# Transposing x on TensorE for three batches, and issuing the first pass's stores from SP

## The chip, the cores and the metric
The kernel runs on one core of a Trainium2 chip. The metric is the device time of one execution in microseconds: 1576.8 us before, the median of three runs (1575.4 to 1581.59). The core has five engines with an instruction stream each: TensorE (PE) for matmuls, VectorE (DVE), ScalarE (ACT), GpSimd (POOL) and SyncE (SP), which here only issues DMAs. A DMA is issued by an instruction in the stream of SP or of ACT and moved by 16 DMA engines. PSUM is the memory that PE writes; SBUF is the other on-chip memory.

## The reference
```python
# attention: x (8, 8, 512, 64), state (8, 8, 32, 64), scale = 1/8
a      = softmax(scale * x @ state^T)          # over the 32 states
xread  = a @ state
a2     = softmax(scale * state @ x^T)          # over the 512 tokens
sread  = a2 @ x
t = concat([xread, sread], axis=2)             # (8, 8, 544, 64) -> (4352, 512)
# gated layer, 512 -> 1536 -> 512
y = (sigmoid(t @ w_gate) * (t @ w_val)) @ w_out
# second layer, 512 -> 2048 -> 512
out = relu(y @ w_in)**2 @ w_out2
```
All arrays are float32; the large weights arrive as 64-bit floats, read as pairs of 32-bit words.

## The kernel before, in words
**Precision.** A float32 operand is split into a high part, rounded to PE's fast format by ACT, and a low part, the difference, by DVE. A product is three matmuls (`mm3`, L190 to L192): high by high, high by low, low by high.

**Weights.** A weight tile comes as raw 64-bit words (`load_raw`, SP, L116, three buffers) and is converted (`convert`): one ACT instruction (L126), five DVE instructions (L128 to L144), an ACT cast (L147) and a DVE subtraction (L148).

**Attention, first half.** For a batch b and a group g of four heads, `load_x` brings x in 32 x 32 blocks by four DMAs of 128 B runs: ACT issues them for batch 0, SP for the others. `a2` transposes the blocks on DVE (L292) into `xf`, so that the 64 features stand on partitions, and splits the result (L293 ACT, L294 DVE). `a3` multiplies it with a diagonal arrangement of the states (PSUM tile `ps_s`), and `a4` makes the softmax over the states: transposes on DVE, exponential on ACT, and the split result `a` (L332, L333). The tiles `xf` and `a1` share one SBUF buffer. The raw x tile `xq` has one buffer.

**The gated layer uses the states' product.** Since xread is a @ state, the product state @ [w_gate, w_val] is formed once for each chunk of two feature tiles (`state_weights`, L452, PSUM pair `ps_g`), copied out (`go`, L456 and L460, three buffers), and stored to DRAM by four DMAs (`store_g`, L468). This is done in two passes over the six chunks: the first (m=0) for batches 0 to 3, the second (m=1) for batches 4 to 7. The first pass's stores are issued by ACT, the second's by SP. For each batch and chunk `load_g` (SP, L512) reads it back, `split_gw` splits it (L520 ACT, L521 POOL), and `front_x` multiplies it with `a` into `psg` and `psv`. A sigmoid (ACT, L537) and a product (DVE, L543) follow, and `back1` accumulates with w_out into `acc`.

**PSUM.** `acc` has four banks, `mm` two, and `at` two. `at` is shared by `ps_st`, `ps_s`, `ps_g` and, later, the transposes of the second softmax (`ps_e`, `ps_sr`, `ps_so`).

**Order.** The work is written in units (batch, feature tile) of six steps. `spread` gives every piece of side work a due step: the attention of batch 0 is written before the first unit, that of batches 1, 2 and 3 in units 1 to 4, 4 to 8 and 8 to 12; the second group of states in unit 23.5. A planner in the framework then orders the instructions of each engine by their priority in the written order and by its own modelled times, and inserts the waits. Each engine runs its list in order, and a DMA issue in that list waits like any other instruction.

The four issuing lines:
```python
# load_x (L258)
(nc.scalar if b == 0 else nc.sync).dma_start(out=..., in_=...)
# store_g (L468)
(nc.sync if m else nc.scalar).dma_start(
    out=to[:, :, i, :], in_=o[NS * r : NS * (r + 1)]
)
```

Of the kernel before, what the change touches and what calls it, by code (L numbers as in the profile page):

```python
# [8 lines left out]
F32 = mybir.dt.float32  # L9
# [9 lines left out]
P = 128  # L19

FC = 2

QB = 4

PAD_L, PAD_R = 144, 160

# [5 lines left out]
def kernel(  # L32
# [21 lines left out]
    nc = tc.nc  # L54
    B, H, S, D = x.shape
    NS = state.shape[2]
# [8 lines left out]
    NT = S // P  # L65
# [19 lines left out]
    at_p = ctx.enter_context(tc.tile_pool(name="at", bufs=2, space=PSUM))  # L85
# [7 lines left out]
    xs_p = one.enter_context(tc.tile_pool(name="xsp", bufs=1, side="right"))  # L93
    aa_p = gen.enter_context(tc.tile_pool(name="aa", bufs=QB, side="right"))
    wr_p = gen.enter_context(tc.tile_pool(name="wr", bufs=2, side="right"))
# [5 lines left out]
    ident = pad_p.tile([P, P], F32, name="ident")  # L101
# [70 lines left out]
    def width(b):  # L172
        return S if b < B else NSTATE
# [11 lines left out]
    }  # L185
    p_dram = {b: dram.tile([P, KD, S], F32, name=f"pd{b}") for b in range(QB)}
    y_dram = {b: dram.tile([P, KD, width(b)], F32, name=f"yd{b}") for b in blocks}
# [19 lines left out]
    xq_p = att.enter_context(tc.tile_pool(name="xq", bufs=1))  # L207
    xn_p = att.enter_context(tc.tile_pool(name="xn", bufs=1))
    xx_p = att.enter_context(tc.tile_pool(name="xx", bufs=2))
    f_p = att.enter_context(tc.tile_pool(name="f2k", bufs=2))  # L210
# [38 lines left out]
    loaded_x, loaded_xn = {}, {}  # L249
    by_pair = x.rearrange("b (g j k) s d -> b g j k s d", g=2, j=2)  # L250

    def load_x(b, g):

        t = xq_p.tile([P, 2, S], F32, tag="xq", name="xq")
        for q in range(4):
            j, e = divmod(q, 2)
            src = by_pair[b, g, j, :, :, 32 * e : 32 * (e + 1)]
            (nc.scalar if b == 0 else nc.sync).dma_start(  # L258
                out=t[32 * q : 32 * (q + 1)].rearrange("i c (J a) -> i (c J) a", a=32),
                in_=src.rearrange("c (J i) a -> i (c J) a", i=32),  # L260
            )
        loaded_x[b, g] = t

# [12 lines left out]
    def group_stages(b, g):  # L276

        v = {}
        busy = b < QB

        def lx():
            load_x(b, g)

        def ln():
            load_xn(b, g)

        def a2(p):
            def run():
                xf = f_p.tile([P, S], F32, tag="xf", name="xf", bufs=1)
                h = xx_p.tile([P, S], F32R, tag="xth", name="xth")  # L290
                l = xx_p.tile([P, S], F32R, tag="xtl", name="xtl")
                nc.vector.transpose(xf, loaded_x[b, g][:, p, :])  # L292
                nc.scalar.copy(out=h, in_=xf)  # L293
                nc.vector.tensor_sub(out=l, in0=xf, in1=h.bitcast(F32))  # L294
                v["xt", p] = (h, l)

            return run
# [104 lines left out]
        def b7():  # L402
# [12 lines left out]

        return {
            "LX": lx, "LN": ln, "LS": ls, "A20": a2(0), "A21": a2(1), "A3": a3, "A4": a4, "SX0": sx(0), "SX1": sx(1),
            "B4": b4, "B5": b5, "B60": b6(0), "B61": b6(1), "B7": b7,
        }
# [8 lines left out]
    def attention(b):  # L428
        gs = [group_stages(b, g) for g in range(2)]
        pick = lambda names: [  # L430
            (lambda: None) if n == "-" else gs[int(n[-1])][n[:-2]] for n in names
        ]
        return [lambda: prep_diag(b), *pick(ORDER_A)], pick(ORDER_B)
# [29 lines left out]
    def store_g(ch, c, m):  # L463
        g, i = divmod(c, 2)
        o = g_out.pop((ch, c, m))
        for r in range(BM):
            to = g_dram[BM * m + r, ch, g].rearrange("(k i n) f -> n k i f", k=2, n=NS)
            (nc.sync if m else nc.scalar).dma_start(  # L468
                out=to[:, :, i, :], in_=o[NS * r : NS * (r + 1)]
            )  # L470

    def conv_out1(f, raw):
        w1[f] = w1_p.tile([P, 2, 512], F32R, name=f"o{f}")
# [2 lines left out]
    def chunk_steps(ch, m, outs):  # L476

        raws = {}  # L480
        jobs = [("p", c) for c in range(NPAIR)] + [("o", f) for f in outs]
        steps = []

        def load(n):
            k, i = jobs[n]
            raws[n] = load_raw(pair_src(ch, i) if k == "p" else row_src(w_out1, i))

        def conv(n):
            k, i = jobs[n]
            if k == "p":  # L490
                conv_gv(ch, i, raws.pop(n))
            else:
                conv_out1(i, raws.pop(n))

        steps += [lambda: load(0), lambda: load(1)]
        for n in range(len(jobs) + 2):
            if n < len(jobs):
                steps.append(lambda n=n: conv(n))
                if n + 2 < len(jobs):
                    steps.append(lambda n=n: load(n + 2))  # L500
            if 1 <= n <= NPAIR:
                steps.append(lambda n=n: state_weights(ch, n - 1, m))
            if 2 <= n <= NPAIR + 1:
                steps.append(lambda n=n: store_g(ch, n - 2, m))
        return steps
# [187 lines left out]
    def front2(b, f):  # L693
        n = width(b)
        ps = mm_p.tile([P, S], F32, tag="mm", name="psi")
        w = need(("i", f)).rearrange("p l (k f) -> p l k f", k=KD)
        for k in range(KD):
            h, l = split_tiles[b, k]
            mm3(ps[:, :n], w[:, 0, k, :], w[:, 1, k, :], h[:, :n], l[:, :n], k == 0, k == KD - 1)
            if k == KD // 2 - 1:  # L700
                step()
        r = g_p.tile([P, S], F32, tag="sg", name="r")
        g32 = g_p.tile([P, S], F32, tag="g32", name="g32")
        nc.scalar.activation(out=r[:, :n], in_=ps[:, :n], func=AF.Relu)  # L704
        nc.vector.tensor_mul(out=g32[:, :n], in0=r[:, :n], in1=r[:, :n])  # L705
        g = split_g(g32, n)
        step()
        return g
# [32 lines left out]
    HALF = NF1 // 2  # L741
    segments = [(b, 0, HALF) for b in range(QB)] + [(b, HALF, NF1) for b in range(QB)]
    segments += [(b, 0, NF1) for b in range(QB, B + 1)]
    units = [(b, f, lo, hi - 1) for b, lo, hi in segments for f in range(lo, hi)]
# [5 lines left out]
    def spread(fns, start, end):  # L750

        for i, fn in enumerate(fns):
            queue.append((STEPS * (start + (end - start) * i / max(len(fns), 1)), len(queue), fn))
# [42 lines left out]
    for ch in range(NCH):  # L796
        spread(chunk_steps(ch, 1, []), 25 + 5 * ch, 30 + 5 * ch)
    for b in range(QB, B):
        start = 33 + 7 * (b - QB)
# [30 lines left out]
    for i, (b, f, lo, hi) in enumerate(units):  # L830
        count[0] = STEPS * i
        g = (front_x if b < B else front_s)(b, f)
# [24 lines left out]
    for i, (b, f) in enumerate(units2):  # L857
# [3 lines left out]
        g = front2(b, f)  # L861
# [35 lines left out]
```

## Time and profile before
| | |
|---|---|
| median of three runs | 1576.8 us |
| the profiled execution | 1575.71 us, span 1573.9 us |
| PE busy | 1494.4 us (95%), 6712 matmuls |
| DVE busy | 865.8 us (55%) |
| ACT busy | 728.7 us (46%) |
| POOL busy | 221.5 us (14%) |
| granted PE clock, mean | 0.974 |
| DMA packets | 185583, of them 112016 under 512 B |

The shares are means over the whole span. The first 280 us hold attention of batches 0 to 3 and the first pass of products; from 840 us on PE runs the second layer with hardly a gap. The page's slices show it: in the first three PE is at two, eight and seven tenths, DVE at seven, nine and eight. An issue of a DMA is not counted as busy time, so ACT's 728.7 us leave out what it spends on issuing.

### The profile page before, as it was taken

What the parts mean: (1) busy time and instruction counts of PE and PEld (TensorE: products, weight loads), DVE (VectorE), ACT (ScalarE), POOL (GpSimd) and SP (SyncE); (2) the same over time, 40 slices, a digit from 0 to 9 for tenths busy, and PEclk for the clock granted to TensorE, in tenths of its full rate; (3) what the DMA queues carried; (4) which work ended last, traced back from release to release, by engine and by line L of the source; (5) the groups of instructions that cost most, each with busy time, mean ns of one, the idle gap of its engine ahead of it and who ended that gap; (6) DMA issues with size and microseconds to landing.
All of it is one profiled execution on the core that took longest, in us unless ns stands there. A gap on an engine that the chain in (4) does not pass through costs nothing.

```text
span 1573.9 us, 19067 instructions
## 1 busy us (share of the span) xinstructions
PE 1494.4 (95%) x6712; PEld 1191.8 (76%) x6712; DVE 865.8 (55%) x1562; ACT 728.7 (46%) x1316; POOL 221.5 (14%) x263
## 2 busy tenths in 40 slices
PE   2879979999999899999999999999999999999998
PEld 1457756777777678888898788888888888888887
DVE  7986689868897665554729942323232232323232
ACT  4665566556676777666425532323232222323222
POOL 1222213312233333434000000000000000000000
PEclk8689989999999899999999999999999999999999
DMA  9764488879986533342845410101010000101000
GB/s 264 225 199 95 108 252 273 291 237 273 290 249 155 167 93 108 94 114 74 310 154 162 125 54 1 54 1 54 1 39 16 27 27 1 54 1 40 0 28 14
DMA packets 185583, 185.80 MB, mean 118 GB/s; under 512 B 112016, under 2 KB 121232, under 8 KB 184464
## 3 DMA queue, kind: packets, MB, share of 16 engines
q1 hardware_dynamic: 169488, 170.96, 35.8%
q10 hardware_dynamic: 16000, 13.64, 3.2%
q8 instruction: 52, 0.85, 0.2%
q14 instruction: 43, 0.35, 0.1%
HBM read 120.59 MB, written 63.96 MB: 117 GB/s over the span
## 4 chain that ended last, share of the span: by engine, by line
PE 85%; DVE 6%; DMA 4%; ACT 3%; issue 1%; POOL 1%; ACTq 1%; SPq 0%; DVEq 0%
PE acc L190 13%; PE acc L191 13%; PE acc L192 13%; PE psi L192 8%; PE psi L190 8%; PE psi L191 8%; PE psg L190 3%; PE psv L190 3%; PE ps_g L452 3%; PE psg L191 3%; PE psg L192 3%; PE psv L191 3%; PE psv L192 3%; DMA gd<-go 2%; DMA gi<-gd 1%
## 5 line engine op out<-in xcount | busy, mean ns | idle before, releaser
L198 DVE TENSOR_TENSOR gl<-g,gh 128x512 fp32r<-128x512 f32 (+1 forms) x252 | 183.5, 728 | 232.9 <-ACT gh L197 219.9
L197 ACT CAST gh<-g 128x512 fp32r<-128x512 f32 (+1 forms) x252 | 150.4, 597 | 250.5 <-PE acc L191 213.4
L705 DVE TENSOR_TENSOR g<-r 128x512 f32<-128x512 f32 (+1 forms) x144 | 95.3, 662 | 234.1 <-ACT r L704 234.0
L521 POOL TENSOR_TENSOR gg<-gi,gg 128x256 fp32r<-128x256 f32 x192 | 164.0, 873 | 420.9 <-ACT gg L520 404.9
L190 PE MATMUL psi<-xh,wi 128*128 128x512 f32 (+1 forms) x576 | 217.7, 378 | 2.1 <-ACT wi L147 2.1
L192 PE MATMUL psi<-xh,wi 128*128 128x512 f32 (+1 forms) x576 | 217.3, 377 | 0.3 <-DVE wi L148 0.3
L191 PE MATMUL psi<-xl,wi 128*128 128x512 f32 (+1 forms) x576 | 217.3, 377 | 0.0
L190 PE MATMUL acc<-wu,gh 128*128 128x512 f32 x544 | 212.1, 390 | 0.8 <-ACT gh L197 0.8
L191 PE MATMUL acc<-wu,gh 128*128 128x512 f32 x544 | 211.8, 389 | 0.0
L704 ACT ACTIVATE r<-psi 128x512 f32<-128x512 f32 (+1 forms) x144 | 82.5, 573 | 275.0 <-PE psi L192 275.0
L192 PE MATMUL acc<-wu,gl 128*128 128x512 f32 x544 | 206.3, 389 | 0.0
L191 PE MATMUL acc<-gl,o 128*128 128x512 f32 (+1 forms) x432 | 164.3, 383 | 0.6 <-DVE gl L198 0.5
L192 PE MATMUL acc<-gh,o 128*128 128x512 f32 (+1 forms) x432 | 163.0, 380 | 0.0
L190 PE MATMUL acc<-gh,o 128*128 128x512 f32 (+1 forms) x432 | 139.1, 382 | 0.1
L190 PEld LDWEIGHTS psi<-xh,wi 128*128 128x128 f32 x576 | 108.4, 188 | 24.2 <-ACT wi L147 3.8
L192 PEld LDWEIGHTS psi<-xh,wi 128*128 128x128 f32 x576 | 108.3, 188 | 20.6 <-DVE wi L148 0.7
L191 PEld LDWEIGHTS psi<-xl,wi 128*128 128x128 f32 x576 | 108.4, 188 | 20.3
L190 PEld LDWEIGHTS acc<-wu,gh 128*128 128x128 f32 x544 | 102.2, 188 | 22.3 <-ACT gh L197 1.7
L192 PEld LDWEIGHTS acc<-wu,gl 128*128 128x128 f32 x544 | 102.2, 188 | 21.3
L191 PEld LDWEIGHTS acc<-wu,gh 128*128 128x128 f32 x544 | 102.2, 188 | 20.6
L190 PE MATMUL psg<-a,gg 128*128 128x512 f32 x192 | 81.4, 424 | 30.8 <-ACT a L332 15.7
L452 PE MATMUL ps_g<-w,st_t 64*128 64x512 f32 x288 | 84.1, 476 | 21.0 <-ACT w L147 13.8
(118 smaller groups left out, 2424.4 us busy)
## 6 DMA issues: line engine op xcount, KB each, us to landing
gi<-gd SPq DMA_DIRECT2D x96, 256.0 KB, 3.3
raw<-in_moe_w_out_dram SPq DMA_DIRECT2D x28, 512.0 KB, 4.3
raw<-in_moe_w_gate_dram SPq DMA_DIRECT2D x48, 256.0 KB, 4.4
raw<-in_moe_w_val_dram SPq DMA_DIRECT2D x48, 256.0 KB, 4.4
gd<-go ACTq DMA_DIRECT2D x96, 128.0 KB, 3.4
wd<-w SPq DMA_DIRECT2D x24, 512.0 KB, 4.3
gd<-go SPq DMA_DIRECT2D x96, 128.0 KB, 3.0
ws<-wd SPq DMA_DIRECT2D x24, 512.0 KB, 8.6
```

Of the source, the lines that this page charges most:

```text
L190: nc.tensor.matmul(ps, lh, rh, start=start, stop=False)
L191: nc.tensor.matmul(ps, lh, rl, start=False, stop=False)
L192: nc.tensor.matmul(ps, ll, rh, start=False, stop=stop)
L197: nc.scalar.copy(out=gh[:, :n], in_=g32[:, :n])
L198: nc.vector.tensor_sub(out=gl[:, :n], in0=g32[:, :n], in1=gh[:, :n].bitcast(F32))
L452: nc.tensor.matmul(ps[j], st_t[rows, l, m, c, :], w[rows, r, :], start=(i == 0), stop=(i == 2))
L521: nc.gpsimd.tensor_sub(out=t[:, 1, g], in0=src, in1=t[:, 0, g].bitcast(F32))
L704: nc.scalar.activation(out=r[:, :n], in_=ps[:, :n], func=AF.Relu)
L705: nc.vector.tensor_mul(out=g32[:, :n], in0=r[:, :n], in1=r[:, :n])
```

## The change
TensorE transposes x for batches 0, 1 and 2 (`NPE = 3`). For these, `load_xt` loads x as token rows by two DMAs of 256 B runs, and `a2` makes four PE transposes of 128 x 128 into a PSUM tile of pool `at`, which ACT and DVE then read in place of `xf`. The other batches keep `load_x` and DVE's transpose. The second load of x (batch 0, second group) and all stores of the first pass are issued by SP; ACT keeps the first load of x alone.

```diff
+NPE = 3
@@ load_x
-            (nc.scalar if b == 0 else nc.sync).dma_start(
+            nc.sync.dma_start(
...
+    def load_xt(b, g):
+
+        t = xq_p.tile([P, 2, NT, P], F32, tag="xq", name="xtok")
+        flat = t.rearrange("p c t n -> p (c t) n")
+        for j in range(2):
+            (nc.scalar if (b, g) == (0, 0) else nc.sync).dma_start(
+                out=flat[:, :, D * j : D * (j + 1)],
+                in_=by_pair[b, g, j].rearrange("c (t p) d -> p (c t) d", p=P),
+            )
+        loaded_x[b, g] = t
@@ group_stages
+        by_pe = b < NPE
+
         def lx():
-            load_x(b, g)
+            (load_xt if by_pe else load_x)(b, g)
...
         def a2(p):
             def run():
-                xf = f_p.tile([P, S], F32, tag="xf", name="xf", bufs=1)
+                if by_pe:
+                    xf = at_p.tile([P, S], F32, tag="at", name="ps_xt")
+                    for t in range(NT):
+                        ts = slice(t * P, (t + 1) * P)
+                        nc.tensor.transpose(xf[:, ts], loaded_x[b, g][:, p, t, :], ident)
+                else:
+                    xf = f_p.tile([P, S], F32, tag="xf", name="xf", bufs=1)
+                    nc.vector.transpose(xf, loaded_x[b, g][:, p, :])
                 h = xx_p.tile([P, S], F32R, tag="xth", name="xth")
                 l = xx_p.tile([P, S], F32R, tag="xtl", name="xtl")
-                nc.vector.transpose(xf, loaded_x[b, g][:, p, :])
                 nc.scalar.copy(out=h, in_=xf)
                 nc.vector.tensor_sub(out=l, in0=xf, in1=h.bitcast(F32))
@@ store_g
-            (nc.sync if m else nc.scalar).dma_start(
-                out=to[:, :, i, :], in_=o[NS * r : NS * (r + 1)]
-            )
+            nc.sync.dma_start(out=to[:, :, i, :], in_=o[NS * r : NS * (r + 1)])
```

## Rows read from the trace of the kernel before

**Rows 1.** The page, busy us of each engine (share of the span), number of instructions.
```profile
PE 1494.4 (95%) x6712; PEld 1191.8 (76%) x6712; DVE 865.8 (55%) x1562; ACT 728.7 (46%) x1316; POOL 221.5 (14%) x263
```

**Rows 2.** Busy us of each engine by stage; then granted clock, DMA share, GB/s.
```profile
8.00:106.00 98.00, 60.01 (x194) 38.10 (x195) 89.95 (x185) 61.05 (x109) 13.99 (x20) 0.77 0.86 247
106.00:150.00 44.00, 40.69 (x159) 32.08 (x159) 29.22 (x44) 27.25 (x48) 13.04 (x19) 0.89 0.45 108
...
200.00:280.00 80.00, 70.14 (x279) 47.45 (x278) 70.75 (x139) 53.77 (x102) 23.83 (x21) 0.94 0.84 264
280.00:480.00 200.00, 200.00 (x839) 145.89 (x838) 167.61 (x293) 122.90 (x222) 53.75 (x67) 1.00 0.86 260
```

**Rows 3.** What PE waited for, 0 to 280 us: total us, times, longest.
```profile
PE psg L190 <- ACT a L332: 15.7, 4, 8.4
PE ps_g L452 <- ACT w L147: 13.8, 2, 7.3
PE psg L190 <- ACT gg L520: 9.5, 1, 9.5
...
PE ps_g L452 <- ACT st_t L234: 2.0, 1, 2.0
```

**Rows 4.** Timeline, 198 to 222 us: start, us, engine, line, instruction, idle before.
```profile
209.12 1.28 DVE L144 CUSTOM_DVE_ANT_0 c<-c,q 128x1024 uint16<-128x1024 uint16 x2
...
212.18 0.62 ACT L147 CAST o<-c 128x512 fp32r<-128x512 f32 x1 [2.87 <-DMA gd<-go]
...
214.62 0.62 ACT L147 CAST w<-c 128x512 fp32r<-128x512 f32 x1 [1.82 <-DMA gd<-go]
...
215.29 1.95 PE L452 MATMUL ps_g<-w,st_t 64*128 64x512 f32 x6 [6.54 <-ACT w L147]
...
219.11 0.63 PE L191 MATMUL psg<-a,gg 128*128 128x512 f32 x1
...
219.54 0.63 PE L192 MATMUL psg<-a,gg 128*128 128x512 f32 x1
```

**Rows 5.** Timeline, 0 to 70 us, ACT's second load of x and what follows.
```profile
14.06 3.80 ACTq L258 DMA_DIRECT2D xq<-in_x_dram  x1
...
18.77 0.62 ACT L147 CAST w<-c 128x512 fp32r<-128x512 f32 x1 [3.52 <-issue]
...
19.42 0.69 DVE L148 TENSOR_TENSOR w<-c,w 128x512 fp32r<-128x512 f32 x1 [2.35 <-ACT w L147]
...
37.58 0.69 DVE L148 TENSOR_TENSOR w<-c,w 128x512 fp32r<-128x512 f32 x1 [0.61 <-ACT w L147]
```

**Rows 6.** DVE's groups by line, 0 to 105 us: busy us, mean ns of one.
```profile
L294 DVE TENSOR_TENSOR xtl<-xf,xth 128x512 fp32r<-128x512 f32 x6 | 5.4, 893 | 0.0
L292 DVE STREAM_TRANSPOSE xf<-xq 128x512 f32<-128x512 f32 x6 | 4.2, 701 | 8.1 <-DMA raw<-in_moe_w_gate_dram 8.1
...
L235 DVE TENSOR_TENSOR st_t<-ps_st,st_t 128x512 fp32r<-128x512 f32 x1 | 0.7, 652 | 0.0
```

**Rows 7.** Timeline of PE around four transposes, 448 to 460 us.
```profile
450.58 0.60 PE L360 MATMUL ps_e<-ident,e 128*128 128x128 f32 x4
450.93 0.48 PE L190 MATMUL psv<-a,gg 128*128 128x512 f32 x1
451.25 0.40 PE L191 MATMUL psv<-a,gg 128*128 128x512 f32 x1
451.48 0.40 PE L192 MATMUL psv<-a,gg 128*128 128x512 f32 x1
```

**Rows 8.** Stores before 106 us; waits of SP and DVE, 8 to 106; DMA issues, 280 to 480.
```profile
L468 ACTq DMA_DIRECT2D gd<-go x48: 309/410/707, 21.0 to 101.1; - x48
...
SPq L116 <- DVE c L128: 28.0, 12, 6.2
...
DVE xf L292 <- DMA raw<-in_moe_w_gate_dram: 8.1, 1, 8.1
...
gd<-go SPq DMA_DIRECT2D x78, 128.0 KB, 3.2
```

## The prediction
> **What bounds the kernel now.** I read the busy line first: TensorE (PE) works 1494.4 of a span of 1573.9 us [rows 1], so the kernel ends when PE has been fed, and only PE's idle time (79.5 us) and its slow clock can give anything back. Then the table by stage [rows 2], to see where that idle time lies: 98.0 - 60.0 = 38 us of it from 8 to 106 us, 3.3 from 106 to 150, 9.9 from 200 to 280, none from 280 to 480. The change acts before 280, so only the first and the third count. In the first, DVE is busy 89.95 of 98 us at a granted clock of 0.77 for PE: DVE is the bound, PE waits for its results. From 106 to 150 it is the other way round, PE 40.7 of 44 and DVE 29.2. Third, PE's own waits up to 280 us [rows 3]: 15.7 us for the attention weights (L332), 13.8 for converted weights (ACT, L147), 9.5 for the loaded product of weights and states (L520) and 2.0 for the second group of states (L234). Last the timeline around the two long ones. At 207 to 215 us ACT is held by the issue of stores: its copies start 2.87 and 1.82 us late behind `gd<-go`, and PE stands for 6.54 us until the copy that ACT starts at 214.62 is done; then it runs at 0.43 us a matmul [rows 4], against 0.23 at the full clock [rows 7]. At 14 to 19 us the same engine is held by the second load of x (one issue of 3.80 us), its copy is 3.52 us late, DVE 2.35 behind it; once more DVE loses 0.61 behind such a copy [rows 5].
>
> **The change part by part.** Durations are of the profiled execution, 1575.7 us with a span of 1573.9; the median of the runs shown, 1576.8, lies 1.1 above, which I add at the end.
>
> *DVE's transposes, first 105 us.* Of the 12 that go, six lie there, 4.2 us in all [rows 6]. DVE has hardly a gap there, so I count all 4.2. The other six (from 105.1 to 147 us) lie where DVE has 15 us free: nothing. The subtraction that follows now reads PSUM. The nearest row of that kind is the states' (L235), 0.65 us against a mean of 0.89 for L294 [rows 6], so 0 to 1.4 us more for six; I take 0, the long ones may be long for another reason.
>
> *ACT's stalls, first 105 us.* DVE's 2.35 and 0.61 [rows 5] go with the issues that hold ACT: 3.0 us. Together the bound engine gains 7.2 us up to the point where PE goes on at 105 us. Bounds: 0, if the order of the work fills the gaps otherwise, and 18, if the 9.5 us wait for L520 [rows 3] is shortened with all of 8.6. What is late next is the same chain: conversion, product, store, load, L520.
>
> *PE's transposes.* A tile takes four. Before, four such transposes stand in PE's stream at 450.58 (the softmax weights, L360): the next matmul starts 0.35 us later, and the one after it 0.09 later than the usual 0.23 [rows 7], so 0.44 us a tile at the full clock. Six tiles fall into PE's 38 idle us before 106 and cost nothing; if that idle time were gone they would cost the same again. Six fall where PE is nearly full: 6 x 0.44 = 2.6 us. Bounds: 0 if they sink into the 3.3 us idle there, and 5.3 at half the clock. A tile also holds one of the two `at` PSUM buffers until DVE has subtracted. I price that at nothing: before 106 us PE has its idle time for it, from 106 to 150 the state products (L452) that use the same buffers don't run.
>
> The rows show four of them overlapped in 0.60 us [rows 7]. The Trainium skill, TensorE: Matmul & The Clock Gate, Part 4 (PE-mode transpose), speaks against the change here: it gives about 275 ns for one transpose inside a kernel. By its price, one after the other, the six tiles on the path would be an estimated 6.6 us and the sum 1569; the trace has four in little more than the time of two of these, and I take the trace.
>
> *Stores of the first pass.* 96 issues leave ACT. 48 of them lie before 106 us, median 0.41 us, 19.7 us in all [rows 8]; the other 48 from 197 on. From 207 on the stall goes: DVE has the converted values at 209.12 + 1.28 = 210.40, so ACT's copy at 214.62 could start 4.2 us earlier [rows 4], and PE with it. 2.3 us of its wait would stay. The slow matmuls after it: about 5 us of PE work from 215.3 to 221.7 at half the clock cost some 2.6 us; whether PE's clock holds over a gap of 2.3 us no row tells, so I take half, 1.4. Sum 5.6; bounds 0 and 10.4 (6.54 + 1.3 + 2.6). The wait of 2.0 for L234 [rows 3] has ACT behind a store too; I count 1.5 (bounds 0 and 2.0).
>
> *The same stores on SP.* SP must now also wait for ACT's copies, and behind the waiting store stand the raw weight loads, the loads of the product and x. Before 106 us SP spends 28.0 us waiting for DVE to give a raw buffer back [rows 8]; that time covers 19.7 us of issues if they fall into it. DVE waits for a raw load once there, 8.1 us at its first instruction, and in the second pass, 280 to 480 us, SP issues 78 such stores with 3.2 us to landing [rows 8] while PE is never idle [rows 2]. I take 0; bounds 0 and 19.7.
>
> *The load of x.* Two DMAs of 256 B runs for four of 128 B runs, half the runs. For batches 1 and 2 SP issues less; for the first batch's second load it issues two DMAs that ACT had. No wait above ends with x landing, so 0; it can shift the first microsecond either way.
>
> Sum: 1575.7 - 7.2 + 2.6 - 5.6 - 1.5 = 1564.0; with 1.1 the median is 1565.
>
> **Rivals.** *The stall rides along to SP.* The stores were late at 207 to 215 us because transfers were slow to be taken, and now SP is held in the same place, and with it the raw loads that DVE needs next; the planner also lays out each engine's order anew, so ACT's early gaps come back elsewhere. For it: SP's loads and the stores would share one queue, and SP's own waits on `gd<-go` exist already. Against it: the second pass of rows 2 and 8. Only DVE's 4.2 and PE's 2.6 remain: 1575.7 - 4.2 + 2.6 + 1.1 = 1575. By the Trainium skill, DMA: Bandwidth & Descriptors, "Issuing engines are not separate DMA queues", this is the one to expect: issuing on several engines saves only the sequencer's time, usually small beside the transfer. Rows 4 show a place where that time was not small.
>
> *The wait at 95 to 105 us goes as well.* PE's 9.5 us there end with a store and a load in series [rows 3]; if the ramp's chain gets ahead of PE, all of it goes: 1565 - 9.5 = 1555. For it: ACT and DVE both lighter. Against: DVE stays over nine tenths busy, so it still comes last.
>
> *SP is late (slower).* Place: SP's queue before 106 us. A store that waits for ACT's copy holds the raw loads, DVE starves, and the 7.2 us are not gained. Price: at most 19.7 us, so 1575.7 + 19.7 + 2.6 - 5.6 - 1.5 + 1.1 = 1592. It makes the kernel slower beyond what can be told from no change (0.5%, 7.9 us here) if more than 12.4 of the 19.7 us reach DVE. For it: 28.0 us of waits in that queue are waits in order. Against: those are free time, and a raw load takes its place a buffer ahead of DVE.
>
> **How the numbers follow.** Forecast 0.52 (own range 1558 to 1573), stall rides along 0.23, the wait goes too 0.13, SP late 0.12. Faster by over 0.5% means under 1568.9: three quarters of the forecast and all of the third, 0.53. Slower means over 1584.7: most of the last, 0.11. The rest, 0.36, is no change. The range 1551 to 1583 takes in the second and third cases and the lower part of the last, and leaves out less than 2 in 10.
>
> **What would show it.** Right: no store on ACT; from 8 to 106 us DVE loses about 4 us of transposes and PE's first product of the third chunk (105 us before) starts about 7 us earlier; PE's wait for L147 falls from 13.8 to some 6; PE from 106 to 150 holds 24 more short matmuls and nothing else; from 280 on the rows are as before, only earlier. Wrong: DVE waits for raw loads in the ramp (SP late); SP rows of 1.5 us an issue around 200 us with PE idle as before (rode along); PE waiting for an `at` buffer before a transpose or a state product, which I priced at nothing; a lower granted clock from 106 to 150.

## The result and the profile after

The changed kernel takes 1549.96 us, the median of four runs (1548.89 to 1554.75), against 1578.14 for the kernel before in the same runs: a ratio of 0.9834, 95% interval 0.9816 to 0.9852. It is 1.7% faster. The forecast was 1565, so the sign was right and the size less than half (11.8 us forecast, 28.2 measured): 15 us are missing from the sum, and the measured time lies 1 us under the range. The profiled execution took 1554.75 us with a span of 1553.0, which is 20.9 less than the 1573.9 of before; where the text speaks of the trace, it is these 20.9 us that have to be explained. The traces show less than the medians because the profiled execution of the changed kernel was the longest of its four, 4.8 us above their median, and that of the kernel before lay 2.4 below its own.

First the busy line of the page, as [rows 1].

```profile
PE 1502.7 (97%) x6760; PEld 1198.6 (77%) x6760; DVE 856.6 (55%) x1550; ACT 724.5 (47%) x1314; POOL 215.2 (14%) x263
```

PE has 48 matmuls more, the 12 tiles' transposes, and 8.3 us more of busy time. Its idle time falls from 79.5 us to 1553.0 - 1502.7 = 50.3, by 29.2; 29.2 - 8.3 = 20.9. So the gain is idle time of PE. The table by stage, with the columns of [rows 2], shows where it went.

```profile
8.00:106.00 98.00, 75.97 (x252) 48.63 (x250) 92.16 (x190) 65.81 (x117) 15.46 (x24) 0.79 0.87 259
106.00:150.00 44.00, 44.00 (x199) 36.45 (x198) 31.48 (x50) 30.25 (x53) 14.93 (x20) 1.00 0.43 103
150.00:200.00 50.00, 49.59 (x212) 35.60 (x210) 41.59 (x77) 34.62 (x65) 9.60 (x12) 1.00 0.76 210
200.00:280.00 80.00, 77.74 (x314) 53.83 (x313) 64.73 (x119) 48.05 (x97) 22.11 (x28) 1.00 0.85 270
280.00:480.00 200.00, 200.00 (x831) 145.57 (x829) 168.86 (x293) 124.77 (x222) 57.45 (x71) 1.00 0.84 250
```

The first column of busy time is PE's, the third DVE's. PE idles 22.0 us before 106 us instead of 38.0, nothing from 106 to 150 instead of 3.3, and 2.3 from 200 to 280 instead of 9.9. DVE is not lighter in the first stage (92.2 us busy, before 90.0): it does other work in the time that the transposes left. From 150 to 200 us, a stage that the prediction did not look at, DVE is busy 41.6 us and DMA moves 210 GB/s; before, the row of that stage was:

```profile
150.00:200.00 50.00, 48.07 (x204) 37.32 (x203) 32.20 (x49) 29.79 (x52) 11.93 (x19) 1.00 0.47 115
```

So work that stood behind 200 us before, weight loads and their conversion, is done there now: DVE starts to convert seven raw weight tiles in this stage (L130), before one (L128). PE's waits up to 280 us, as [rows 3]:

```profile
PE ps_g L474 <- ACT w L149: 5.6, 3, 3.3
...
PE psg L192 <- ACT gg L540: 0.6, 1, 0.6
PE psg L192 <- ACT a L354: 0.4, 1, 0.4
```

All three long waits are shorter, two of them nearly gone: converted weights 13.8 to 5.6 us, the loaded product 9.5 to 0.6, and the one that the change was not expected to touch, the attention weights `a`, 15.7 to 0.4.

When this turns into a lead is read from the ends of the blocks, the end of the last DVE copy `y<-acc` of each (us from the span's start):

| block of the first pass | before | after | lead |
|---|---|---|---|
| first | 119.8 | 120.2 | -0.4 |
| second | 162.1 | 156.8 | 5.3 |
| third | 205.4 | 204.1 | 1.3 |
| fourth | 267.5 | 251.0 | 16.5 |

The last row, for the kernel before and then the one after; from here on the start of this last copy stands for the end of a block:

```profile
266.82 0.68 DVE L611 COPY y<-acc 128x512 f32<-128x512 f32 x1
```
```profile
250.33 0.68 DVE L631 COPY y<-acc 128x512 f32<-128x512 f32 x1
```

Of the 20.9 us, then, nothing is there when the ramp ends, where the prediction had its largest term, and 16.5 are there at 250 us; in the second pass, at the copy that ends batch 4's block (518.60 us, before 539.35), all are. PE's granted clock from 8 to 106 us was much the same in the two executions (0.77 and 0.79), so the first row is not a matter of the clock. The idle time before 106 us was not turned into finished blocks but into work done ahead: attention of later batches and, from it, room for the fourth chunk's weights.

### The profile page after: what moved, and what is told of

It reads as the page before. It is cut to its first block, busy times and chain, and to the rows that moved or that the text cites. A ratio compares the mean times of both kernels' runs of the same rounds, so it can differ in the third digit from the quotient of the medians.

```text
span 1553.0 us, 19161 instructions
## 1 busy us (share of the span) xinstructions
PE 1502.7 (97%) x6760; PEld 1198.6 (77%) x6760; DVE 856.6 (55%) x1550; ACT 724.5 (47%) x1314; POOL 215.2 (14%) x263
## 4 chain that ended last, share of the span: by engine, by line
PE 86%; DVE 5%; DMA 4%; ACT 2%; issue 1%; SPq 1%; POOL 0%; DVEq 0%; ACTq 0%
PE acc L193 13%; PE acc L192 13%; PE acc L194 13%; PE psi L194 8%; PE psi L192 8%; PE psi L193 8%; PE psv L192 3%; PE psg L192 3%; PE ps_g L474 3%; PE psv L193 3%; PE psv L194 3%; PE psg L193 3%; PE psg L194 3%; DMA raw<-in_moe_w_val_dram 2%; DMA gd<-go 1%
## 5 line engine op out<-in xcount | busy, mean ns | idle before, releaser
L541 POOL TENSOR_TENSOR gg<-gi,gg 128x256 fp32r<-128x256 f32 x192 | 157.6, 840 | 399.6 <-ACT gg L540 392.1
L194 PE MATMUL acc<-gh,o 128*128 128x512 f32 (+1 forms) x432 | 163.1, 379 | 0.0
L192 PE MATMUL acc<-gh,o 128*128 128x512 f32 (+1 forms) x432 | 143.2, 386 | 0.7 <-ACT gh L199 0.7
L193 PEld LDWEIGHTS acc<-gl,o 128*128 128x128 f32 x432 | 81.3, 188 | 21.8 <-DVE gl L200 3.5
L192 PEld LDWEIGHTS acc<-gh,o 128*128 128x128 f32 x432 | 80.5, 190 | 20.3 <-issue 2.4
```

The source lines that it names most:

```text
L192: nc.tensor.matmul(ps, lh, rh, start=start, stop=False)
L193: nc.tensor.matmul(ps, lh, rl, start=False, stop=False)
L194: nc.tensor.matmul(ps, ll, rh, start=False, stop=stop)
L541: nc.gpsimd.tensor_sub(out=t[:, 1, g], in0=src, in1=t[:, 0, g].bitcast(F32))
```

## The buffer that the transposes held

The tiles `xf` (x transposed, L289) and `a1` (softmax weights in `a4`) share one SBUF buffer. `a1`'s last reader is the subtraction L333. So the first DVE transpose of a group of heads can't start before L333 of the group ahead. DVE's timeline of the kernel before shows it, one pair a group (start, us, engine, line, instruction):

```profile
121.79 0.69 DVE L333 TENSOR_TENSOR a<-a,a 128x512 fp32r<-128x512 f32 x1 [0.69 <-ACT a L332]
122.52 0.71 DVE L292 STREAM_TRANSPOSE xf<-xq 128x512 f32<-128x512 f32 x1
...
143.86 0.68 DVE L333 TENSOR_TENSOR a<-a,a 128x512 fp32r<-128x512 f32 x1
144.58 0.71 DVE L292 STREAM_TRANSPOSE xf<-xq 128x512 f32<-128x512 f32 x1
...
162.02 0.67 DVE L333 TENSOR_TENSOR a<-a,a 128x512 fp32r<-128x512 f32 x1
162.73 0.71 DVE L292 STREAM_TRANSPOSE xf<-xq 128x512 f32<-128x512 f32 x1
```

A transpose stands right behind each L333, about 20 us apart: the groups' attention goes through one after the other. The profile names no wait here, since DVE has other work and the planner has put the transpose where the buffer comes free. In the changed kernel the transposed tile is in PSUM. PE's timeline:

```profile
90.82 0.80 PE L192 MATMUL psg<-a,gg 128*128 128x512 f32 x1 [0.55 <-ACT gg L540]
...
98.14 1.25 PE L309 MATMUL ps_xt<-ident,xtok 128*128 128x128 f32 x8 [2.15 <-DMA xtok<-in_x_dram]
...
106.23 0.60 PE L309 MATMUL ps_xt<-ident,xtok 128*128 128x128 f32 x4
106.58 0.48 PE L192 MATMUL psg<-a,gg 128*128 128x512 f32 x1
```

And DVE's, in the same kernel:

```profile
107.04 0.81 DVE L355 TENSOR_TENSOR a<-a,a 128x512 fp32r<-128x512 f32 x1
...
129.52 1.20 DVE L355 TENSOR_TENSOR a<-a,a 128x512 fp32r<-128x512 f32 x1 [0.38 <-ACT a L354]
131.25 0.70 DVE L312 STREAM_TRANSPOSE xf<-xq 128x512 f32<-128x512 f32 x1
```

L309 of batch 2's second group, the sixth, at 106.23 comes ahead of the L355 (the old L333) of the fourth group at 107.04: the groups overlap. Batch 3 still uses `xf`, and its first transpose still stands behind an L355, but at 131.25 instead of 162.73 us. This is a correlation only; whether the buffer, the shorter DVE work or the stores made the gain, the experiments below tell.

## The experiments

Two theories. *Buffer*: the gain comes from taking `xf` out of the buffer of `a1`. *Work* (the prediction's): it comes from DVE's transposes and ACT's issues that are gone. Ratios are to the kernel before on the same chip, with 95% intervals.

### The parts of the change alone

**Stores alone.** The kernel before, with all stores on SP.
```diff
-            (nc.sync if m else nc.scalar).dma_start(
+            nc.sync.dma_start(
```


> The kernel before with the first pass's stores on SP and nothing else (x as before, its first batch loaded by ACT). Theory A, ACT's stalls: the stores are what held ACT, so this alone brings most of the gain: 207 to 215 us without the 6.5 us wait, ratio 0.990 to 0.994. Theory B, the order: the gain comes from where the third chunk's successor stands in the order of the engines; here it still starts behind 16 units, as before, so DVE stays half idle from 106 to 200 us and crowded from 200 to 280: ratio 0.995 to 1.001. Theory C, SP late: DVE waits for raw loads before 106 us, ratio over 1.003.

Measured 1574.48 us, ratio 0.9975 (0.9961 to 0.9988): some 4 us. The waits of PE up to 280 us and the stage from 200 on:
```profile
PE psg L190 <- ACT a L332: 15.6, 5, 9.6
PE psg L190 <- ACT gg L518: 8.7, 1, 8.7
PE ps_g L452 <- ACT w L147: 7.6, 1, 7.6
```
```profile
200.00:280.00 80.00, 77.39 (x308) 53.37 (x307) 70.77 (x140) 57.24 (x106) 17.76 (x19) 0.98 0.88 271
```
The stall at 207 to 215 us is gone as forecast: the wait for converted weights falls by 6.2 us and PE is busy 77.39 us of this stage instead of 70.14. The fourth block ends 7.9 us earlier, at 258.96. But the first had ended 2.7 later, at 121.88, and the kernel gains only 4. At the copy that ends batch 4's block nothing of the 7.9 us is left (539.26, before 539.35). What takes them back was not settled.

**PE transposes alone,** with their 256 B loads; the stores and the second load of x stay on ACT.
```diff
-            nc.sync.dma_start(out=to[...], in_=o[...])
+            (nc.sync if m else nc.scalar).dma_start(out=to[...], in_=o[...])
...
-            (nc.scalar if (b, g) == (0, 0) else nc.sync)
+            (nc.scalar if b == 0 else nc.sync)
```


> The changed kernel with all stores of the first pass and both first loads of x back on ACT, so PE's transposes alone. Theory A: DVE gains 4.2 us, PE pays 2.6: ratio 0.998 to 1.001, and ACT's stalls stay. Theory B: in this order the fourth chunk's product stands behind 13 units instead of 16, so most of the 26 us come from here, ratio 0.985 to 0.991, with DVE over 0.7 busy from 150 to 200 us and PE without the long wait behind 200.

Measured 1554.7 us, ratio 0.9848 (0.9826 to 0.9871), at the lower edge of what was expected. This part is nearly the whole change.

**Second load of x alone.** The kernel before, with that load on SP.
```diff
-            (nc.scalar if b == 0 else nc.sync).dma_start(
+            (nc.scalar if (b, g) == (0, 0) else nc.sync).dma_start(
```


> The kernel before with only the second load of x (first batch, second group) moved from ACT to SP, four DMAs as before. Theory A: ACT's copy at 18.8 us is 3.5 us earlier and DVE's gap of 2.35 us goes: ratio 0.998 or a little less. Theory B: the order is that of the kernel before, so no more than these 2.4 us can come; a later wait may take them: 0.998 to 1.000.

Measured 1578.43 us, ratio 1.0001 (0.9986 to 1.0016): nothing. DVE's wait for ACT's converted `w` before 106 us falls from 4.6 to 1.9 us, so the stall of [rows 5] is gone, and no time comes of it.

**Transposes and stores,** the change without the second load.
```diff
-            (nc.scalar if (b, g) == (0, 0) else nc.sync)
+            (nc.scalar if b == 0 else nc.sync)
```


> The changed kernel with the second load of x back on ACT alone, so transposes and stores without that load. Theory A: 2 to 3 us slower than the changed kernel, ratio to the kernel before 0.985 to 0.986. Theory B: the fourth chunk stands behind 12 units as in the changed kernel, so the ratio is that of the changed kernel, 0.983, within 0.002.

Measured 1551.85 us, ratio 0.9831 (0.981 to 0.9851), the same as the whole change, and within the intervals the same as the transposes alone.

### The buffer by itself

**DVE transposes into another buffer.** The kernel before; PE transposes nothing, the loads and the stores are as they were. Only the tile that DVE writes for batches 0 to 2 moves to the buffer of the second softmax, which isn't needed yet.
```diff
-                xf = f_p.tile([P, S], F32, tag="xf", name="xf", bufs=1)
+                if b < 3:
+                    xf = f_p.tile([P, S], F32, tag="et", name="xo", bufs=1)
+                else:
+                    xf = f_p.tile([P, S], F32, tag="xf", name="xf", bufs=1)
```


> The kernel before with DVE's transposes and all issues as they were; only the transposed tile of batches 0 to 2 lies in another SBUF buffer, one that the second softmax needs later, instead of the one that it shares with a1. Buffer theory: before, each group's first transpose starts right behind the last reader of a1 of the group ahead, so freeing it is what the change really does: ratio 0.982 to 0.988, as with PE's transposes alone. DVE theory (the transposes' time): nothing is taken off DVE, 0.998 to 1.002.

Measured 1560.74 us, ratio 0.9887 (0.9868 to 0.9906). With not one instruction taken off an engine, two thirds of the gain is there, a little less than the 0.982 to 0.988 expected. PE's wait for `a` and the stage from 150 us:
```profile
PE psg L190 <- ACT a L335: 1.7, 1, 1.7
```
```profile
150.00:200.00 50.00, 50.00 (x201) 35.85 (x200) 40.97 (x74) 33.47 (x62) 10.21 (x13) 1.00 0.72 196
```
Both look like the changed kernel (0.4 us; DVE 41.59 busy, 210 GB/s), not like the one before (15.7 us; 32.20, 115 GB/s).

**The lock put back.** The changed kernel, where ACT copies each transposed tile from PSUM into the shared buffer. It adds 12 copies of ACT.
```diff
                         nc.tensor.transpose(xf[:, ts], ...)
+                    xc = f_p.tile([P, S], F32, tag="xf", name="xc", bufs=1)
+                    nc.scalar.copy(out=xc, in_=xf)
+                    xf = xc
```


> The changed kernel, PE's transposes, loads and stores kept, but ACT copies the transposed tile from PSUM into an SBUF tile that shares its buffer with a1, as xf did; 12 copies of some 0.6 us more on ACT. Buffer theory: the groups are in series again, the fourth chunk stands behind 15.7 units, and most of the gain goes: ratio to the kernel before 0.993 to 1.003. DVE theory: DVE is as light as in the changed kernel, the ratio stays at 0.983 to 0.988.

**The same copies into a free buffer.** The control, equal but for the tag.
```diff
-                    xc = f_p.tile([P, S], F32, tag="xf", name="xc", bufs=1)
+                    xc = f_p.tile([P, S], F32, tag="et", name="xc", bufs=1)
```


> As the kernel with the extra copy into a1's buffer, instruction for instruction, but the copy goes to the buffer that nothing else uses yet. Buffer theory: the gain of the changed kernel but for ACT's 7 us of copies, most of them hidden: ratio 0.983 to 0.988. If this one is as slow as its pair, the copies were the cost and not the buffer.

Measured 1580.31 us, ratio 1.0013 (1.0 to 1.0026), for the first and 1549.05, ratio 0.9818 (0.9795 to 0.9842), for the second. The two execute the same instructions, but for four more loads of ACT's tables (1.28 us each) with the lock, and differ by 31 us, more than the change gains. ACT's group of copies up to 280 us, first with the lock, then free (busy, mean ns | idle before, releaser):
```profile
L311 ACT COPY xc<-ps_xt 128x512 f32<-128x512 f32 x12 | 7.0, 583 | 4.0 <-DVE a L358 2.1 <-DVE xtl L319 0.8 <-PE psv L193 0.6
```
```profile
L311 ACT COPY xc<-ps_xt 128x512 f32<-128x512 f32 x12 | 7.0, 583 | 1.1 <-DVE xtl L319 1.1
```
With the lock ACT waits for L358, the old L333; in its timeline the copy follows it by 0.09 us:
```profile
103.43 0.69 DVE L358 TENSOR_TENSOR a<-a,a 128x512 fp32r<-128x512 f32 x1
104.21 0.59 ACT L311 COPY xc<-ps_xt 128x512 f32<-128x512 f32 x1 [0.81 <-DVE a L358]
```
The wait itself is small; what it orders is larger. PE's longest wait up to 280 us and the stage from 150 us, with the lock, look like those of the kernel before again:
```profile
PE psg L192 <- ACT a L357: 18.2, 3, 8.9
```
```profile
150.00:200.00 50.00, 47.31 (x196) 36.41 (x195) 31.97 (x50) 29.82 (x51) 11.93 (x18) 0.97 0.41 106
```
and free, that stage is as in the changed kernel:
```profile
150.00:200.00 50.00, 49.10 (x210) 35.18 (x209) 42.82 (x79) 35.45 (x68) 10.95 (x14) 1.00 0.77 216
```
The 12 copies, 7.0 us of ACT, cost nothing that shows. But the ramp holds only a part of the 31 us. The fourth block's last copy starts at about 252 us with the lock and at 245.23 free, 7 us apart, and even with the lock it is well ahead of the kernel before (266.82). The copy that ends batch 4's block shows 33 us:
```profile
546.69 0.65 DVE L634 COPY y<-acc 128x512 f32<-128x512 f32 x1
```
```profile
513.53 0.68 DVE L634 COPY y<-acc 128x512 f32<-128x512 f32 x1
```
Between the two points PE idles 15.1 us with the lock and 5.0 free, and executes 1124 matmuls against 1097: some work that is done ahead with the free buffer is still to do there. How much of those 26 us is this work and how much the other order in which the planner laid out the second pass was not separated.

**The chunk placed earlier instead.** The planner takes the fourth chunk's products (`ps_g`) earlier when the attention ahead of them is earlier: in the traces the first of its four products starts at 189.07 us, behind 17 units, in the kernel before, and at 155.11, behind 13.5, in the changed one (counted by the matmuls into `psg` and `psv`, twelve a unit). This kernel is the one before with the due steps of the last three chunks of the first pass two units earlier, while the attention is locked as before.
```diff
-        spread(chunk_steps(ch, 0, outs[ch]), 11.5 + 4 * (ch - 3), 15.5 + 4 * (ch - 3))
+        spread(chunk_steps(ch, 0, outs[ch]), 9.5 + 4 * (ch - 3), 13.5 + 4 * (ch - 3))
```


> The kernel before with the due steps of the fourth to sixth chunk 2 units earlier: the fourth chunk's first product then stands behind 12 units, as in the changed kernel, while the attention of batches 1 to 3 stays in series behind the shared buffer. If the place of that chunk alone is what counts (DVE used from 150 to 200 us): ratio 0.985 to 0.990. If the attention in series is what counts: 0.995 to 1.001.

Measured 1574.49 us, ratio 0.998 (0.9967 to 0.9992). The earlier due steps bring 0.2%. PE still waits for `a`:
```profile
PE psg L190 <- ACT a L332: 18.0, 5, 8.1
```
But the run did less than it was meant to: only the first of the chunk's products came early, behind 13.5 units, and the next waited until 17.5 units were done (194.46 us; 198.56 in the kernel before, 166.18 in the changed one).
```profile
168.71 0.96 PE L452 MATMUL ps_g<-w,st_t 64*128 64x512 f32 x3
...
194.46 0.96 PE L452 MATMUL ps_g<-w,st_t 64*128 64x512 f32 x3
```
So it shows that earlier due steps do not bring the chunk forward while the attention is locked. What the whole chunk would be worth earlier, with the lock in place, stays open.

**All runs together.** PE's wait for ACT's `a` up to 280 us follows the buffer in every trace. Where the transposed tile shares it with `a1` (the kernel before, stores alone, second load alone, lock, early due steps) it is 15.1 to 18.2 us; in the nine other kernels of this document it is at most 1.7. DVE is busy 32.0 to 36.8 of the 50 us from 150 on in the first five and 40.6 to 42.8 in the others. Since the planner draws the order anew for each edit, a time alone proves less: below, edits that leave the buffer as it is move it by 0.8%. The buffer alone is not far above that with 1.1%; the pair, with 2%, is.

### What the transposes cost, how the parts add, how many batches

**Twice the transposes.** The changed kernel, with each of the four transposes of a tile made twice into the same place: 48 more on PE.
```diff
                         nc.tensor.transpose(xf[:, ts], ...)
+                        nc.tensor.transpose(xf[:, ts], ...)
```


> The changed kernel with each group of four PE transposes made twice into the same tile, so 48 more transposes; the planner's order stays much the same (fourth chunk behind 13 units, 12 in the changed kernel). By the price of the prediction, 0.44 us a tile with the early half hidden, 2 to 4 us slower than the changed kernel: ratio to the kernel before 0.984 to 0.987. If transposes cost 275 ns each on the path: 6 to 13 us slower, 0.987 to 0.992.

Measured 1561.61 us, ratio 0.9915 (0.9892 to 0.9938), 0.8% above the changed kernel: more than the 48 could cost in PE's stream at the full clock, 12 x 0.44 = 5.3 us by [rows 7]. The ratio falls into the range expected for 275 ns each, but not for that reason: up to the fourth block they cost nothing that shows, for it ends at 245.90 us against 250.33 (granted clock 0.86 from 8 to 106 us, against 0.79, which may be part of the lead). The loss comes later, where no transpose of x stands; PE's largest gap from 280 to 480 us is
```profile
460.86 0.50 PE L192 MATMUL psg<-a,gg 128*128 128x512 f32 x1 [2.04 <-ACT sg L558]
```
The clock is not the reason: from 480 to 520 us, 0.91 was granted, in the changed kernel 0.87. The planner had laid the second pass out in another order. So this run does not measure the price of a transpose.

**Other buffer and stores on SP,** the kernel before with these two edits together, to see whether the parts add up without PE's transposes.
```diff
+                if b < 3: xf = f_p.tile([P, S], F32, tag="et", name="xo", bufs=1)
...
+            nc.sync.dma_start(out=to[...], in_=o[...])
```


> DVE's transposes and the kernel before's loads of x, the transposed tile of batches 0 to 2 in a buffer of its own, and the first pass's stores on SP: the changed kernel without PE's transposes. Buffer theory: between the buffer alone (0.9887) and the changed kernel, 0.984 to 0.988. If PE's transposes are worth their 6 us beside the stores as they were without them, 0.986; if the stores bring the same gain as on the kernel before (0.0025), 0.986 as well; under 0.983 the transposes on PE cost more than they bring.

Measured 1570.5 us, ratio 0.9964 (0.9948 to 0.998). This missed: the two together are worse than the buffer alone (0.9887). One part of it is in the ramp, where DVE now waits for x:
```profile
DVE xo L295 <- DMA raw<-in_moe_w_gate_dram: 7.9, 1, 7.9
DVE xo L295 <- DMA xq<-in_x_dram: 3.9, 1, 3.9
```
The first block ends 6 us later than with the buffer alone (123.22 against 117.18). The load of x stands in SP's queue, where the stores now stand as well and wait 11.0 us for ACT's copies before 106 us; that the one delays the other is likely but was not tried by itself. The lag is still 5.5 us at the fourth block's end (257.29 against 251.82) and 14.1 at the end of batch 4's block (536.42 against 522.32). From the fourth block to this one it takes 279.1 us, stores alone 280.3 and the lock some 295, against 272.5 in the kernel before, 270.5 with the buffer alone and 268.3 in the changed kernel. The three long ones have all the stores on SP, but so has the changed kernel; the cause of this second half stays open.

**Four and eight batches on PE.** The changed kernel.
```diff
-NPE = 3
+NPE = 4
```


> The changed kernel with the fourth batch's x transposed on PE too (NPE = 4): its first half of attention also leaves the shared buffer, the fourth chunk stands behind 11 units. Buffer theory: PE waits little for attention weights by now, so little is left, ratio to the kernel before 0.980 to 0.984. Price of four more tiles on a full PE: 1.8 us.

```diff
-NPE = 3
+NPE = 8
```


> The changed kernel with all eight batches transposed on PE. Past 280 us PE has no idle time, so 20 more tiles than in the changed kernel cost 20 x 0.44 = 8.8 us less what idle time around 480 to 600 us takes: ratio to the kernel before 0.984 to 0.989. If the attention of batches 4 to 7 gains from the freed buffer, less: 0.980 to 0.984.

Measured 1548.96 us, ratio 0.984 (0.9816 to 0.9863), and 1559.46, ratio 0.9895 (0.9876 to 0.9914), just above what was expected. A fourth batch changes nothing, though it frees the buffer for one batch more. With all eight, PE loses time between 480 and 840 us:
```profile
480.00:840.00 360.00, 344.75 (x1760) 288.70 (x1761) 212.39 (x427) 217.22 (x418) 99.47 (x108) 0.97 0.48 146
```
It is busy 344.75 us there against 351.16 in the changed kernel, with waits of 5.2 us for the loaded product and 3.8 for `sp` (L571). Which part of these is the transposes' and which is order wasn't tried. Neither kernel beats the changed one by more than the intervals.

## Why the prediction was half right

**What bounds the kernel: right, but read too narrowly.** PE's idle time was the thing to win, and 28.4 of the 29.2 us lie before 280. But the longest of PE's waits, the 15.7 us for `a`, was listed and then passed over, without asking what `a` itself waits behind. And DVE's load was taken as the bound of the first stage, though DVE is as busy there after the change, with PE idle 16 us less.

**The step that failed** is the second half of *DVE's transposes, first 105 us*: "The other six (from 105.1 to 147 us) lie where DVE has 15 us free: nothing." The transposes were priced as time of an engine, where what they held was a buffer. Their starts, each right behind an L333, stand in the trace from which their duration was read; [rows 6] give only its sum and mean. The buffer alone is worth 0.9887 in the kernel before; put back into the changed kernel, sharing it again takes all of the gain (1.0013 against 0.9818), in part behind the ramp. The prediction asked whether the tile's new place in PSUM would hold anything up, and never what its old place had held up.

**DVE's 4.2 us and ACT's 3.0: mis-sized.** What the prediction calls the first product of the third chunk, at 105.15 us, is the second half of that chunk's first unit. The first half starts at 90.34 before and 90.82 after, the second at 105.15 and 103.23: 1.9 us earlier for a forecast 7.2.
```profile
90.34 0.50 PE L190 MATMUL psg<-a,gg 128*128 128x512 f32 x1
...
105.15 0.80 PE L190 MATMUL psg<-a,gg 128*128 128x512 f32 x1 [9.48 <-ACT gg L520]
```
```profile
101.39 0.76 PE L192 MATMUL ps_s<-xth,diag 128*128 128x512 f32 x1 [1.99 <-DVE xtl L316]
...
103.23 0.63 PE L192 MATMUL psg<-a,gg 128*128 128x512 f32 x1
```
Between the halves PE now does attention of later groups. The time that left DVE and ACT was filled with other work. The load alone took the stall away and gained nothing, and stores alone left DVE's wait for `w` as it was (4.6 to 4.9 us). What PE transposes add over the free buffer, 0.9887 to 0.9848, is some 6 us, and holds DVE's 12 transposes and the longer runs of the load together; the intervals touch, so this is a size and not a proof.

**The subtraction from PSUM: 0, right.** L316 takes 677 ns a tile from PSUM in the mean; L294 took 808 from SBUF in the first 280 us.

**PE's transposes, 2.6 us on the path: too high.** The forecast had six tiles there. Since the groups run ahead, ten of the twelve lie before 106 us in PE's idle time. The tile at 106.23 lets the next matmul start 0.35 us later, as [rows 7] had it; at a granted clock of 0.50 four take 1.12 us, at 89.15, in that idle time. The figure of the Trainium skill, TensorE: Matmul & The Clock Gate, Part 4 (PE-mode transpose), of about 275 ns for one, fits the duration of one here (273 ns, the median of 48), but not their price in a stream: after four the next matmul starts 0.35 us behind the first. The PSUM hold was priced at nothing. PE waited 2.2 us for ACT's `go` ahead of a transpose, and 1.4 us ahead of a state product for DVE's subtraction (L316) to release a transposed tile. Another 2.2 us it waited for x to land. That any of these made the kernel longer was not shown.

**The stores, 5.6 and 1.5 us: the place was right, the sum too high.** Alone they are worth 4 us, in the change 0.2% or nothing (0.9848 without them, 0.9831 with them). With the transposes on PE there is hardly a stall left to remove: PE's wait for converted weights (the old L147) up to 280 us is 5.5 us with the stores still on ACT and 5.6 in the changed kernel. The Trainium skill, DMA: Bandwidth & Descriptors, "Issuing engines are not separate DMA queues", says that issuing from several engines saves only the time of the sequencer that issues, usually small beside the transfer; that moving the stores from ACT to SP changed the time by no more than 0.25% here (0.9975) agrees.

**SP and the second load, 0: right.** DVE waits for raw weights 8.3 us at its first instruction and 1.4 us more in the ramp. Around 190 us SP does stand for long, as the first rival had it:
```profile
189.43 5.06 SPq L490 DMA_DIRECT2D gd<-go  x4
```
but PE has no wait there. The stall rode along, and it harmed nobody.

**The rivals.** The stall rides along (1575) and SP is late (1592) did not come. "The wait at 95 to 105 us goes as well" (1555) is closest in time, and its wait fell from 9.5 to 0.6 us, but not for its reason. The chain did not get ahead of PE: ACT's copy that PE waits for starts at 101.64 us instead of 104.69, and PE has other work until then. And with the buffer freed and DVE no lighter, the wait is gone too; with the stores alone it is 8.7.

## What to carry to other kernels

When an operation moves to another engine or memory, list the buffers it gives back, and for each look in the timeline at what starts right behind the buffer's last reader: such a pair, repeated group after group, may be a lock, though the profile may name no wait for it. A lock on one buffer can be tried without moving any work, by giving the tile another buffer; do that before the work is moved. And where a planner draws the order anew for each edit, small parts don't add up (the stores were worth -0.25%, -0.2% and, with the other buffer, +0.8%), so a part is to be tested in the kernel it will live in.

## What the runs showed that I had not expected

- A DVE subtraction that reads PSUM was no slower than one from SBUF: 677 ns against 808 in the mean, for 128 x 512. The medians are nearly the same, 678 ns and, over the whole span, 687: a few long ones make the difference.
- Four stores held SP for 5.06 us in one place (one issue alone 3.28) and 1.75 in the next, for the same 128 KB each; the median issue on ACT before 106 us was 0.41.
- From 106 to 150 us PE was granted 1.00 instead of 0.89 and had no idle time there (44.0 of 44 us busy, before 40.69). With the buffer alone it was granted 1.00 as well, at 41.00 us busy. In the changed kernel the waits that went thus gave back more than their own length: 199 matmuls in that stage, 8 of them the short transposes, against 159.
